# Half of the first layer of the last 1024 tokens as seven products in place of eight

## The chip, the cores and the metric

The kernel runs on one core of a Trainium2 chip. Its time is the device time of one execution in microseconds (us). The engines have short names: PE is TensorE (PEld its weight loads), DVE is VectorE, ACT is ScalarE, POOL is GpSimd, and SP is the engine that issues the DMAs.

## The reference

Attention with a sliding window of 32 tokens to either side, for 8 sequences of 576 tokens with 8 heads of 64, is followed by a feed-forward layer over all 4608 tokens:

```python
scores = scale * np.matmul(q, k.transpose(0, 1, 3, 2))
mask = np.abs(pos[:, None] - pos[None, :]) <= window
attn = softmax(np.where(mask, scores, -1e9))
x = np.matmul(attn, v)                  # -> (4608, 512)
h = x @ w_in                            # 512 -> 2048
r = np.maximum(h, 0.0)
out = (s * (r * r) + b) @ w_out         # 2048 -> 512
```

## The kernel before

**Tiles and stages.** The 4608 tokens are cut into 9 blocks of 512 (`NG`). The first three blocks are cut further (`SPLIT`), the last six are not. Attention goes by units of 128 keys (two tiles of 64); the last five sequences run as one long chain of units. A unit takes scores on PE (L828), an exponential on ACT (L856), a mask on DVE (L860), the products with v on PE (L886), and the normalization on DVE (L908 and L910). For the later units SP then transposes the normalized tile into `XT` by DMA (L934). `XT` holds the attention's result with the model's dimension on the partitions; it is a ring of 1536 tokens.

**First layer.** `s1(m, f0)` makes one f-tile (128 of the 2048 columns of w_in) of block `m`: four matmuls of 512 columns into one of the two banks `W` (L1149), a rectification by ACT from PSUM into `R1` (L1156), and, for each two f-tiles, a square by DVE into `GT` (L1162). There are two buffers `GT`, for blocks with even and odd numbers.

**Second layer.** `second(x)` already works by seven products in place of eight (the Strassen-Winograd scheme): the squares of a block and w_out are each taken as a 2 x 2 matrix, sums of the parts are made by DVE (L1198 for the squares, `weight_sums` once for w_out), and each product is two groups of eight matmuls of 256 columns (L1206) into the banks `O`. DVE adds each product, scaled by s, to the rows of the output (L1222), and SP stores them (L1231). The last block (`apart`) also uses the banks `SC`, which the attention no longer needs.

**The order of the work.** The kernel records each piece of work as a task with its engine, an estimated cost, what it reads and writes, and a due time `key`. A planner (`_Graph.plan`) then takes tasks one after the other, the earliest possible start first and the earlier key among equals, and so fixes one order for each engine, which the engine follows strictly. `_Graph.emit` adds the waits on semaphores. The keys come from a plan of stages: in stage x the first layer of block x (`P1`) alternates with the second layer of block x - 1 (`P2`); after the last stage comes the second layer of block 8. `due(c, u)` gives the key of an attention unit, some 14 us ahead of the block that needs it.

**Loads.** SP's queue holds the loads of q, k and v of the later sequences, the transposes of q and k (after POOL has cast them to bf16, L780, the transposes at L796), the transposes into `XT` (L934) and the stores (L1231), in the planner's order. v is cast to bf16 by ACT (L613) or DVE (L614) in turn. At the end `flag` tests that all row sums of the attention lie in a safe range, and only otherwise a slow general program runs.

The functions that the change touches, with the lines that the profile names:

Of the kernel before, what the change touches and what calls it, by code (L numbers as in the profile page):

```python
# [5 lines left out]
F32 = mybir.dt.float32  # L6
# [48 lines left out]
KEPT = 8  # L55
STIR = {("turn", 0, "q"): 7, ("scores", 0): 3, ("turn", 1, "q"): 2, ("turn", 1, "k"): 1, ("turn", 2, "q"): 1, ("turn", 2, "k"): 1,
# [267 lines left out]
def bass_sliding_window_symmetric__then__act_starrelu_kernel(  # L324
# [23 lines left out]
    with ExitStack() as es:  # L348
# [85 lines left out]
        for x in range(NG + 1):  # L434
            ms = BLOCKS[x] if x < NG else []
            n2 = 14 if x else 0
            work = sum(16 * c1(m) for m in ms)
            long, start = work + n2 * 0.874, at
            for m in ms:
                PH.append(at)  # L440
                share = long * 16 * c1(m) / work
                for ft in range(16):
                    P1[m, ft] = at + ft / 16.0 * share
                at += share
            for i in range(n2):
                P2[x - 1, i] = start + (i + 0.5) / n2 * long + (DELAY if x < NG else 0.0)
            at = start + long
# [23 lines left out]
        def due(c, u):  # L471
# [5 lines left out]
            before = PH[blk] - PH[blk - 1] if blk > 0 else 4.0  # L477
            return PH[blk] - 14.0 - (1.0 - f) * before
# [646 lines left out]
        def place(m):  # L1125

            return TBLK[m][0] // 512 % 2, TBLK[m][0] % 512

        def gt_res(gs, fc, c0, n):
            return [("GT", gs, fc, c) for c in range(c0 // 32, (c0 + n) // 32)]  # L1130
# [4 lines left out]
        def s1(m, f0):  # L1135
# [22 lines left out]
            if both and not half:  # L1158
# [3 lines left out]
            add("dve", lambda e: e.tensor_tensor(GT[gs][:, f1:f1 + nf, g0:g0 + nt], rr, rr, ALU.mult),  # L1162
                130 + 0.55 * nf * nt, reads=[("R1", rb, x) for x in range(2 if both else 1)],
                writes=[r for g in range(nf) for r in gt_res(gs, f1 + g, g0, nt)], key=key)

# [15 lines left out]
        def g_part(x, y, t):  # L1181
            return GT[x % 2].rearrange("p (g y) c -> p g y c", y=2)[:, :, y, HT * t:HT * t + HT]

        def g_res(x, y, t, halves=(0, 1)):
            return [r for h in halves for g in range(4 * h, 4 * h + 4) for r in gt_res(x % 2, 2 * g + y, HT * t, HT)]

        def second(x):
# [57 lines left out]
            for h in (0, 1):  # L1245
                k = P1[max(BLOCKS[x][-1], NE), 10] if h == 0 else key[0] - 1.0
# [57 lines left out]
        for x in range(1, NG):  # L1304
            for m in BLOCKS[x]:
                attend(m)
                for ft in range(0, 16, group(m)):
                    s1(m, ft)
            second(x - 1)
        second(NG - 1)  # L1310

        def flag():
# [3 lines left out]
            low, both = STG[0][:, 0:NU * H], STG[1][:, 0:NU * H]  # L1316
            low_res, both_res = stg_res(0, 2 * DM), stg_res(2 * DM, 2 * DM)
# [245 lines left out]
```

## Time and profile before

| | us |
|---|---|
| median of 3 runs | 307.87 |
| lowest, highest | 306.24, 308.62 |
| the profiled execution's own time | 309.07 |
| its span, from the first to the last instruction | 307.3 |

The profile shows one execution. Its page gives busy times by engine, a strip of 40 slices, the DMA queues, the chain of work that ended last, and the costliest groups of instructions. A row of a group gives the kernel's line, the engine, the operation, output and inputs, shapes and count, then busy time and the mean duration of one, then the idle time before them with what ended it. Matmuls overlap, so their single durations in a timeline are longer than what each adds; the chain of waits shows what a group adds.

### The profile page before, as it was taken

What the parts mean: (1) busy time and instruction counts of PE and PEld (TensorE: products, weight loads), DVE (VectorE), ACT (ScalarE), POOL (GpSimd) and SP (SyncE); (2) the same over time, 40 slices, a digit from 0 to 9 for tenths busy, and PEclk for the clock granted to TensorE, in tenths of its full rate; (3) what the DMA queues carried; (4) which work ended last, traced back from release to release, by engine and by line L of the source; (5) the groups of instructions that cost most, each with busy time, mean ns of one, the idle gap of its engine ahead of it and who ended that gap; (6) DMA issues with size and microseconds to landing.
All of it is one profiled execution on the core that took longest, in us unless ns stands there. A gap on an engine that the chain in (4) does not pass through costs nothing.

```text
span 307.3 us, 8802 instructions
## 1 busy us (share of the span) xinstructions
PE 292.1 (95%) x3822; PEld 211.1 (69%) x3849; DVE 230.2 (75%) x394; ACT 164.3 (53%) x261; POOL 63.3 (21%) x77
## 2 busy tenths in 40 slices
PE   8986899999999999999999999999899999999994
PEld 2455778798888887666766675666566666666784
DVE  4665798998769697977699897796876776566673
ACT  3754876695888564757465446543654433333300
POOL 5153568100000242037005400370000000000000
PEclk9999999999999999999999999999999999999999
DMA  6999999999793979999899879897803110200223
GB/s 182 316 265 319 310 288 359 285 246 229 172 194 94 246 136 163 251 236 210 158 286 200 158 178 258 191 184 141 237 17 87 53 47 22 83 30 6 69 70 107
DMA packets 118616, 54.43 MB, mean 177 GB/s; under 512 B 91232, under 2 KB 114400, under 8 KB 118576
## 3 DMA queue, kind: packets, MB, share of 16 engines
q1 hardware_dynamic: 118576, 53.85, 73.4%
q8 instruction: 31, 0.51, 0.7%
q14 instruction: 9, 0.07, 0.1%
HBM read 36.70 MB, written 9.44 MB: 150 GB/s over the span
## 4 chain that ended last, share of the span: by engine, by line
PE 78%; SPq 8%; DMA 5%; DVE 3%; issue 2%; POOL 2%; ACT 1%; POOLq 0%
PE w L1149 35%; PE o L1206 31%; DMA stg<-in_k_dram 4%; PE avn L886 4%; SPq L761 2%; PE sc L1206 2%; PE sc L828 2%; POOL nat L780 2%; SPq L796 1%; DMA vst<-in_v_dram 1%; SPq L650 1%; PE avn L917 1%; SPq L620 1%; SPq L577 1%; DVE kt L699 1%
## 5 line engine op out<-in xcount | busy, mean ns | idle before, releaser
L1149 PE MATMUL w<-xt,win 128*128 128x512 bf16 (+4 forms) x805 | 137.6, 312 | 3.8 <-issue 1.6
L1156 ACT ACTIVATE r<-w 128x512 bf16<-128x512 f32 (+2 forms) x148 | 86.2, 586 | 85.0 <-PE w L1149 82.5
L1149 PEld LDWEIGHTS w<-xt,win 128*128 128x128 bf16 x832 | 73.9, 98 | 34.9 <-ACT r L1156 1.3
L1162 DVE TENSOR_TENSOR gt<-r 128x1024 bf16<-128x1024 bf16 (+3 forms) x100 | 62.3, 629 | 31.4 <-ACT r L1156 30.9
L1206 PE MATMUL o<-wout,gt 128*128 128x256 bf16 x528 | 66.5, 273 | 0.0
L1206 PEld LDWEIGHTS o<-wout,gt 128*128 128x128 bf16 x528 | 50.9, 98 | 13.0
L780 POOL CAST nat<-stg 128x1024 bf16<-128x1024 f32 (+2 forms) x28 | 32.4, 1158 | 80.2 <-DMA stg<-in_q_dram 65.3
L856 ACT ACTIVATE ex<-sc 128x1024 bf16<-128x1024 f32 (+1 forms) x29 | 29.6, 1022 | 17.6 <-PE avn L886 16.3
L1206 PE MATMUL o<-tw,gt 128*128 128x256 bf16 x272 | 34.6, 273 | 0.0
L1222 DVE SCALAR_TENSOR_TENSOR outs<-o,sb,cvec 128x512 f32<-128x512 f32 (+1 forms) x36 | 25.7, 715 | 8.2 <-PE o L1206 7.9
L1206 PEld LDWEIGHTS o<-tw,gt 128*128 128x128 bf16 x272 | 26.3, 98 | 7.4
L1222 DVE SCALAR_TENSOR_TENSOR outs<-o,sb,outs 128x512 f32<-128x512 f32 (+1 forms) x27 | 19.3, 715 | 8.4 <-PE o L1206 8.3
L1198 DVE TENSOR_TENSOR gt<-gt 128x1024 bf16<-128x1024 bf16 (+1 forms) x26 | 23.7, 913 | 0.2
L860 DVE TENSOR_TENSOR ex<-ex,mask 128x1024 bf16<-128x1024 bf16 (+1 forms) x29 | 21.5, 740 | 1.4 <-ACT ex L856 0.9
L910 DVE TENSOR_TENSOR xn<-avn,rec 128x512 bf16<-128x512 f32 (+1 forms) x31 | 21.2, 685 | 0.5
L886 PE MATMUL avn<-vb,ex 64*64 64x65 bf16 x944 | 19.9, 197 | 0.3
L886 PEld LDWEIGHTS avn<-vb,ex 64*64 64x64 bf16 x944 | 12.9, 107 | 9.1 <-issue 4.7
L1206 PE MATMUL o<-tw,gsum 128*128 128x256 bf16 x136 | 17.6, 273 | 0.0
L1206 PEld LDWEIGHTS o<-tw,gsum 128*128 128x128 bf16 x136 | 13.1, 98 | 3.9
L1198 DVE TENSOR_TENSOR gsum<-gt 128x1024 bf16<-128x1024 bf16 x18 | 13.0, 721 | 0.4
L925 ACT COPY xt<-avn 128x512 bf16<-128x512 bf16 (+2 forms) x18 | 9.4, 531 | 4.9 <-PE avn L917 4.9
L828 PE MATMUL sc<-qt,kt 64*64 64x128 bf16 x440 | 11.7, 216 | 0.0
(132 smaller groups left out, 232.1 us busy)
## 6 DMA issues: line engine op xcount, KB each, us to landing
out_dram<-outs SPq DMA_DIRECT2D x32, 256.0 KB, 3.0
vst<-in_v_dram SPq DMA_DIRECT2D x28, 256.0 KB, 4.2
stg<-in_k_dram SPq DMA_DIRECT2D x24, 256.0 KB, 6.4
stg<-in_q_dram SPq DMA_DIRECT2D x5, 1024.0 KB, 6.5
stg<-in_moe_w_in_dram SPq DMA_DIRECT2D x8, 512.0 KB, 7.4
stg<-in_moe_w_out_dram SPq DMA_DIRECT2D x8, 512.0 KB, 7.3
stg<-in_q_dram SPq DMA_DIRECT2D x4, 512.0 KB, 8.9
stg<-in_k_dram SPq DMA_DIRECT2D x4, 512.0 KB, 8.9
```

The source lines that it names most:

```text
L780: (lambda e, dst=dst, src=src: e.tensor_copy(dst, src)),
L828: fns = [lambda e, pr=pr, x=x, b=b, j=j, hp=hp: e.matmul(SC[64 * x:64 * x + 64, hp, pr * 128:pr * 128 + 128], lhsT=k_tile(b, pr, j)[64 * h ...
L856: add("act", lambda e, dst=flat_dst, src=flat_src: e.activation(dst, src, AF.Exp, bias=0.0, scale=0.125), 190 + 0.833 * 512 * len(hs), rea ...
L860: add("dve", lambda e, flat=flat, mask=mask: e.tensor_tensor(flat, flat, mask, ALU.mult), 130 + 0.53 * 512 * len(hs), reads=[("E", ei, hp, ...
L886: return [lambda e: e.matmul(av[64 * x:64 * x + 64, h, 0:D + 1], lhsT=buf[64 * g:64 * g + 64, h % 2, h // 2, c:c + 64], rhs=VB[64 * g:64 * ...
L910: add("dve", lambda e: e.tensor_tensor(XN[xi][0:p1, :].rearrange("p (a c) -> p a c", a=H), av[0:p1, :, 0:D], REC[ri][0:p1, :].rearrange("p ...
L1149: add("pe", [lambda e, g=g, kc=kc: e.matmul(wt[:, g, :], lhsT=WIN_BF[:, kc, (f0 + g) * 128:(f0 + g + 1) * 128], rhs=XT[:, kc, t0 % XR:t0 % ...
L1156: add("act", lambda e: e.activation(rt, wt, AF.Relu, bias=0.0, scale=1.0), 190 + 0.833 * ng * nt, reads=[("W", wb)], writes=[("R1", rb, ha ...
L1162: add("dve", lambda e: e.tensor_tensor(GT[gs][:, f1:f1 + nf, g0:g0 + nt], rr, rr, ALU.mult), 130 + 0.55 * nf * nt, reads=[("R1", rb, x) fo ...
L1198: add("dve", lambda e: e.tensor_tensor(dst, x, y, op), 1240.0 if half is None else 690.0, reads=reads, writes=writes, key=k)
L1206: add("pe", [lambda e, g=g, j=j, dst=dst: e.matmul(dst, lhsT=lhs[:, g, 128 * j:128 * j + 128], rhs=rhs[:, g, :], start=first and g == 0 an ...
L1222: add("dve", lambda e, src=src, dst=dst, other=other: e.scalar_tensor_tensor(dst, src, SB128[:, 0:1], other, ALU.mult, ALU.add), 200 + 1.0 ...
```

## The change

For the f-tiles 8 to 15 of the last two blocks (7 and 8, 1024 tokens), the first layer is now made by `quad_group`, four times. A quad is two f-tiles by two blocks: the two halves of the model's dimension and two f-tiles of w_in make a 2 x 2 matrix, and the two halves and two blocks of `XT` make the other. Seven products of two matmuls each give the four results. Products 1, 6, 7 and 4 accumulate one on the other in one PSUM bank (`chain`), and after each of the first three ACT copies the partial sum to SBUF (`keep`). Products 2, 5 and 3 go to other banks (`other`, `side`); DVE adds a kept sum to them (`join`). ACT then rectifies, and DVE squares as before. `quad_sums` makes four sums of w_in (into `NAT`, keyed 8 us before the quads, and not before the attention product of the fifth unit from the end) and four of `XT` (into `VST`, when all attention is done), all by DVE.

The f-tiles 0 to 7 of both blocks stay with `s1`. All quads stand in stage 7, interleaved with the second layer of block 6, so stage 8 has only eight f-tiles left, and block 8 gets a third buffer of squares of its own, in the space of the staging buffers `STG`. The banks of the attention (`AVN`, `SC`) serve as chain and side banks, so the attention must be finished before; `due` gives the units of the last two blocks earlier keys. The sums of the last block's second layer and `flag` move to other buffers or keys.

The core of the diff:

```diff
@@ -53,6 +53,16 @@
 EV2 = ("act", "dve", "act", "dve", "act")
 
 KEPT = 8
+QUADS = 4
+FASTEST = 16 - 2 * QUADS
+TRAIL = 2.0
+FIN = 0.75
+LEAD = 7.0
+TURNS = ("dve", "dve") * QUADS
+HELD = 4
+AHEADS = 8.0
+AFTER = 5
+SUMS = ("dve", "dve")
 STIR = {("turn", 0, "q"): 7, ("scores", 0): 3, ("turn", 1, "q"): 2, ("turn", 1, "k"): 1, ("turn", 2, "q"): 1, ("turn", 2, "k"): 1,
         ("turn", 3, "q"): 1, ("turn", 3, "k"): 1, ("scores", 2): 1, ("scores", 3): 1, ("av", 0): 5, ("turn", "t"): 2}
 OUTSIDE = -1.0e38
@@ -434,16 +444,21 @@
         for x in range(NG + 1):
             ms = BLOCKS[x] if x < NG else []
             n2 = 14 if x else 0
-            work = sum(16 * c1(m) for m in ms)
+            fts = range(FASTEST) if x == NG - 1 else range(16)
+            quads = 28 * c1(NM - 1) / 4 * QUADS if x == NG - 2 else 0.0
+            work = sum((FASTEST if x >= NG - 2 else 16) * c1(m) for m in ms) + quads
             long, start = work + n2 * 0.874, at
             for m in ms:
                 PH.append(at)
-                share = long * 16 * c1(m) / work
-                for ft in range(16):
-                    P1[m, ft] = at + ft / 16.0 * share
+                share = long * ((FASTEST if x >= NG - 2 else 16) * c1(m) + quads) / work
+                for ft in fts:
+                    P1[m, ft] = at + ft / len(fts) * share * (FIN if x == NG - 1 else 1.0)
+                    if quads:
+                        P1[m, ft] = at + (ft * c1(m) if ft < FASTEST else FASTEST * c1(m) + (ft - FASTEST) / (16 - FASTEST) * quads) * long / work
+                        P1[m + 1, ft] = P1[m, ft] + 0.05
                 at += share
             for i in range(n2):
-                P2[x - 1, i] = start + (i + 0.5) / n2 * long + (DELAY if x < NG else 0.0)
+                P2[x - 1, i] = start + (i + 0.5) / n2 * long + (TRAIL if x == NG - 2 else DELAY if x < NG else 0.0)
             at = start + long
         PH.append(P2[NG - 1, 0] - 0.5 * n2 / 14 * 0.874)
         PH.append(at)
@@ -475,6 +490,8 @@
             blk = next(x for x in range(NM) if TBLK[x][0] + TBLK[x][1] > tok)
             f = (tok - TBLK[blk][0]) / TBLK[blk][1]
             before = PH[blk] - PH[blk - 1] if blk > 0 else 4.0
+            if blk >= NM - 2:
+                return PH[NM - 3] - LEAD + (tok - TBLK[NM - 2][0]) / 1024 * (P1[NM - 2, FASTEST] - PH[NM - 3])
             return PH[blk] - 14.0 - (1.0 - f) * before
 
 
@@ -1124,9 +1141,16 @@
 
         def place(m):
 
-            return TBLK[m][0] // 512 % 2, TBLK[m][0] % 512
+            return home(TBLK[m][0] // 512), TBLK[m][0] % 512
+
+        def home(x):
+            return 2 if x == NG - 1 else x % 2
+
+        GTS = GT + [STGS[:, 0:4096].bitcast(BF16).rearrange("p (f c) -> p f c", f=16)]
 
         def gt_res(gs, fc, c0, n):
+            if gs == 2:
+                return [("STG", 4 * fc + c) for c in range(c0 // 128, (c0 + n - 1) // 128 + 1)]
             return [("GT", gs, fc, c) for c in range(c0 // 32, (c0 + n) // 32)]
 
         def group(m):
@@ -1159,9 +1183,116 @@
                 return
             f1, nf = (f0 - 1, 2) if both else (f0, ng)
             rr = R1[rb][:, 0:nf * nt].rearrange("p (g c) -> p g c", g=nf)
-            add("dve", lambda e: e.tensor_tensor(GT[gs][:, f1:f1 + nf, g0:g0 + nt], rr, rr, ALU.mult),
+            add("dve", lambda e: e.tensor_tensor(GTS[gs][:, f1:f1 + nf, g0:g0 + nt], rr, rr, ALU.mult),
                 130 + 0.55 * nf * nt, reads=[("R1", rb, x) for x in range(2 if both else 1)],
                 writes=[r for g in range(nf) for r in gt_res(gs, f1 + g, g0, nt)], key=key)
+
+        quad, weight = {}, {}
+
+        def quad_sums():
+
+            x0, key = TBLK[NM - 2][0], P1[NM - 2, FASTEST]
+            c0 = x0 % XR
+            assert c0 + 1024 <= XR
+
...
+                for dst, a, b, op, reads, i in ((S1, a21, a22, ALU.add, [], 0), (S2, S1, a11, ALU.subtract, own[0], 1),
+                                                (S3, a11, a21, ALU.subtract, [], 2), (S4, a12, S2, ALU.subtract, own[1], 3)):
+                    eng = SUMS[part]
+                    add(eng, lambda e, dst=dst, a=a, b=b, op=op: e.tensor_tensor(dst, a, b, op),
+                        510.0 * n if eng == "pool" else 140.0 + 141.0 * n,
+                        reads=Win + reads, writes=own[i], key=P1[NM - 2, ft] - AHEADS + 0.1 * i,
+                        waits=[land["av", LONG, seq_units(LONG) - AFTER]])
+
...
+            B11, B12, B21, B22 = (XT[:, 2 * lower:2 * lower + 2, c0 + 512 * t:c0 + 512 * t + 512] for lower in (0, 1) for t in (0, 1))
+            T1, T2, T3, T4 = T
+            early, late_ = xt_res(x0, x0 + 512), xt_res(x0 + 512, x0 + 1024)
+            for dst, a, b, reads, i in ((T1, B12, B11, early + late_, 0), (T2, B22, T1, late_ + [("VST", 0)], 1),
+                                        (T3, B22, B12, late_, 2), (T4, B21, T2, early + [("VST", 1)], 3)):
+                add("dve", lambda e, dst=dst, a=a, b=b: e.tensor_tensor(dst, a, b, ALU.subtract), 700.0,
+                    reads=reads, writes=[("VST", i)], key=key - 2.0 + 0.1 * i)
+
...
+        def quad_group(i):
+
+            f0, z = FASTEST + 2 * i, i % 2
+            m = NM - 2
+            name, bank = (("AVN", AVN), ("SC", SC))[z]
+            wb = count["w"] % 2
+            count["w"] += 1
+            ra, rb = count["r"] % NR1, (count["r"] + 1) % NR1
+            count["r"] += 2
+            chain, side, other = ((name, 0), bank[:, 0, :]), ((name, 1), bank[:, 1, :]), (("W", wb), W[:, wb, :])
+            key = [P1[m, f0] + (P1[m, f0 + 1] - P1[m, f0]) * x / 3.5 for x in range(8)]
...
+            def product(n, dst, first, k):
+                (lhs, lres), (rhs, rres) = weight[i // HELD][n], quad[n]
+                add("pe", [lambda e, kk=kk: e.matmul(dst[1], lhsT=lhs(i % HELD, kk), rhs=rhs[:, kk, :], start=first and kk == 0, stop=(kk == 1),
+                                                     skip_group_check=True) for kk in (0, 1)],
+                    c1(m) * 500.0, reads=lres + rres, writes=[dst[0]], key=k, slack=XTS if n < 3 else 0.0)
+
+            def keep(dst, res, k):
+                add("act", lambda e: e.copy(dst, chain[1]), 617.0, reads=[chain[0]], writes=res, key=k)
+
+            def join(src, mine, res, r, half, k):
+                add("dve", lambda e: e.tensor_tensor(R1[r][:, 512 * half:512 * half + 512], src[1], mine, ALU.add), 660.0,
+                    reads=[src[0]] + res, writes=[("R1", r, half)], key=k)
+
+            def rectify(dst, src, reads, r, halves, k):
+                add("act", lambda e: e.activation(dst, src, AF.Relu, bias=0.0, scale=1.0), 190 + 0.833 * 512 * len(halves),
+                    reads=reads, writes=[("R1", r, x) for x in halves], key=k)
+
+            def square(r, t, eng, k):
+                gs = home(NG - 2 + t)
+                rr = R1[r][:, :].rearrange("p (g c) -> p g c", g=2)
+                add(eng, (lambda e: e.activation(GTS[gs][:, f0:f0 + 2, :], rr, AF.Square, bias=0.0, scale=1.0)) if eng == "act" else
+                    (lambda e: e.tensor_tensor(GTS[gs][:, f0:f0 + 2, :], rr, rr, ALU.mult)), 700.0 if eng == "dve" else 1040.0,
+                    reads=[("R1", r, x) for x in (0, 1)], writes=[x for g in (0, 1) for x in gt_res(gs, f0 + g, 0, 512)], key=k)
+
+            A, C = R1[ra], R1[rb]
+            product(1, chain, True, key[0])
+            keep(p1, p1r, key[0])
+            product(2, other, True, key[1])
+            product(6, chain, False, key[2])
+            keep(u2, u2r, key[2])
+            join(other, p1, p1r, ra, 0, key[1])
+            product(5, side, True, key[3])
+            product(7, chain, False, key[4])
+            keep(u3, u3r, key[4])
+            join(side, u3, u3r, rb, 1, key[4])
+            product(3, side, False, key[5])
+            join(side, u2, u2r, rb, 0, key[5])
+            product(4, chain, False, key[6])
+            rectify(A[:, 0:512], A[:, 0:512], [("R1", ra, 0)], ra, (0,), key[3])
+            rectify(C[:, :], C[:, :], [("R1", rb, x) for x in (0, 1)], rb, (0, 1), key[6])
+            rectify(A[:, 512:1024], chain[1], [chain[0]], ra, (1,), key[6])
+            square(rb, 1, TURNS[2 * i], key[7])
+            square(ra, 0, TURNS[2 * i + 1], key[7])
 
         def weights_part(y, c0):
             return WOUT_BF.rearrange("p (g y) c -> p g y c", y=2)[:, :, y, c0:c0 + HN]
@@ -1179,10 +1310,10 @@
                     reads=reads, writes=writes, key=key)
 
         def g_part(x, y, t):
-            return GT[x % 2].rearrange("p (g y) c -> p g y c", y=2)[:, :, y, HT * t:HT * t + HT]
+            return GTS[home(x)].rearrange("p (g y) c -> p g y c", y=2)[:, :, y, HT * t:HT * t + HT]
 
         def g_res(x, y, t, halves=(0, 1)):
-            return [r for h in halves for g in range(4 * h, 4 * h + 4) for r in gt_res(x % 2, 2 * g + y, HT * t, HT)]
+            return [r for h in halves for g in range(4 * h, 4 * h + 4) for r in gt_res(home(x), 2 * g + y, HT * t, HT)]
 
         def second(x):
 
@@ -1243,7 +1374,7 @@
                 s2, s4 = (STG[i].bitcast(BF16).rearrange("p (g c) -> p g c", g=8) for i in (4, 5))
                 rs2, rs4 = (stg_res(2 * DM * i, 2 * DM) for i in (4, 5))
             for h in (0, 1):
-                k = P1[max(BLOCKS[x][-1], NE), 10] if h == 0 else key[0] - 1.0
+                k = P1[max(BLOCKS[x][-1], NE), 10 if x < NG - 1 else FASTEST - 1] if h == 0 else key[0] - 1.0
                 h11, h12, h21, h22 = (g_res(x, y, t, (h,)) for t in (0, 1) for y in (0, 1))
                 total(s1, a21, a22, ALU.add, h21 + h22, [("GSUM", h)], k, h)
                 if apart:
@@ -1304,8 +1435,13 @@
         for x in range(1, NG):
             for m in BLOCKS[x]:
                 attend(m)
-                for ft in range(0, 16, group(m)):
+                for ft in range(0, 16 if x < NG - 2 else FASTEST, group(m)):
                     s1(m, ft)
+            if x == NG - 2:
+                attend(NM - 1)
+                quad_sums()
+                for i in range(QUADS):
+                    quad_group(i)
             second(x - 1)
         second(NG - 1)
 
@@ -1313,8 +1449,8 @@
 
             key = PH[-2] - 24.0
             seen = RECS.rearrange("p u h -> p (u h)")
-            low, both = STG[0][:, 0:NU * H], STG[1][:, 0:NU * H]
-            low_res, both_res = stg_res(0, 2 * DM), stg_res(2 * DM, 2 * DM)
+            low = both = VST[:, 4, :, :].rearrange("p h d -> p (h d)")[:, 0:NU * H]
+            low_res = both_res = [("VST", 4)]
             add("dve", lambda e: e.tensor_scalar(low, seen, LEAST, None, ALU.is_ge), 450,
                 reads=[("REC", i) for i in range(NU)], writes=low_res, key=key)
             add("dve", lambda e: e.scalar_tensor_tensor(both, seen, 1.0 / LEAST, low, ALU.is_le, ALU.mult), 450,
```

23 lines of the change are left out of this document (added).

## The prediction, made before the result was known

> **What bounds the kernel now.** I read the page first, then the windows of the last 100 us, the chain of waits, and the timelines of the engines.
>
> ```profile
> span 307.3 us, 8802 instructions
> ```
>
> ```profile
> core 0: us, PE busy (x) PEld busy (x) DVE busy (x) ACT busy (x) POOL busy (x), PEclk, DMA share, GB/s
> ...
> 210.00:220.00 10.00, 8.68 (x147) 5.80 (x147) 6.92 (x12) 4.96 (x8) 0.00 (x0) 1.00 0.79 190
> 220.00:230.00 10.00, 9.95 (x111) 6.49 (x110) 7.41 (x13) 4.80 (x9) 0.00 (x0) 1.00 0.24 59
> 230.00:240.00 10.00, 9.79 (x147) 6.73 (x147) 7.37 (x13) 4.90 (x7) 0.00 (x0) 1.00 0.26 67
> 240.00:250.00 10.00, 9.77 (x87) 6.43 (x87) 7.39 (x13) 3.58 (x6) 0.00 (x0) 1.00 0.21 55
> 250.00:260.00 10.00, 9.95 (x68) 6.56 (x68) 6.36 (x11) 3.61 (x7) 0.00 (x0) 1.00 0.07 24
> ```
>
> From 216 us on TensorE is the bound: 98 to 99% busy at a granted clock of 1.00, with VectorE at 64 to 74%, ScalarE at 36 to 49%, GpSimd idle and DMA at 0.07 to 0.26. So a matmul taken away there is time saved, as long as VectorE and ScalarE can carry what replaces it. The one hole near the change lies in 210 to 220. The chain names it:
>
> ```profile
> 211.05 3.83 DMA vst<-in_v_dram
> 214.91 0.62 ACT vb L613
> 215.52 0.51 ACT r L1156
> ...
> 217.99 0.25 PE avn L886 x16
> ...
> 218.79 0.81 PE w L1149 x3
> ...
> 228.18 1.73 PE w L1149 x8
> 229.91 0.87 PE o L1206 x8
> ```
>
> ```profile
> 216.07 1.04 PE L1149 MATMUL w<-xt,win 128*128 128x512 bf16 x4 [1.05 <-ACT r L1156]
> ```
>
> A load of v is issued after the last transposes of k, ScalarE's cast stands waiting for it, the rectifications queue behind the cast, and TensorE finds both W banks full: 1.05 us lost. The later rows give the unit prices: an attention unit takes TensorE from 217.99 to 218.79, 0.8; a first-layer matmul of 512 columns takes 1.73/8 = 0.216 us of TensorE, a first-layer group of four 0.87, a second-layer group of eight 0.87.
>
> **The products.** For f-tiles 8 to 15 of blocks 7 and 8 the change removes 2 x 8 x 4 = 64 such matmuls and adds 4 quads x 7 products x 2 = 56 of the same shape (0.43 us a product). That is 8 x 0.216 = 1.73 us less of TensorE. Weight loads fall by the same eight and are hidden anyway (64 to 67% busy above, while TensorE computes). This is the whole direct gain.
>
> **What ScalarE gets.** It loses 16 rectifications and gets, per quad, three copies of a partial sum out of PSUM (512, to f32), two rectifications of 512 and one of 1024.
>
> ```profile
> L1156 ACT ACTIVATE r<-w 128x512 bf16<-128x512 f32 x45 | 26.7, 597 | 41.5 <-PE w L1149 40.3 <-PE avn L1324 1.1
> L856 ACT ACTIVATE ex<-sc 128x1024 bf16<-128x1024 f32 x3 | 3.1, 1023 | 2.0 <-PE avn L886 1.9
> ```
>
> An f32 copy isn't in the trace: at least 0.60 (same size, bf16 out), at most 1.02 (twice the elements); I take 0.60, since only the output type differs. Four quads: 12 x 0.60 + 8 x 0.60 + 4 x 1.02 = 16.1 us, 6.5 more than the 16 x 0.60 it replaces; at 1.02 a copy, 21.1. ScalarE has half its time free. What matters is the order inside a quad: products 1, 6, 7, 4 accumulate in one bank, and the next may write only when the copy of the last is made. In the built order at least a second-layer group and one product stand between two of these, 0.87 + 0.43 = 1.30 us, against a copy of 0.60 (margin about 0.65) or 1.02 (0.25). So I cost the copies at nothing; the second-layer groups hide them. Without that cover each would cost up to 0.60, twelve of them 7 us.
>
> **What VectorE gets.** It keeps as many squares and gets 12 joins (PSUM plus f32), 4 sums of w_in and 4 of the attention's result, each of 1024 in bf16.
>
> ```profile
> L1162 DVE TENSOR_TENSOR gt<-r 128x1024 bf16<-128x1024 bf16 x23 | 15.9, 691 | 16.1 <-ACT r L1156 15.9
> L1222 DVE SCALAR_TENSOR_TENSOR outs<-o,sb,cvec 128x512 f32<-128x512 f32 x11 | 8.2, 745 | 3.5 <-PE o L1206 3.5
> L1198 DVE TENSOR_TENSOR gsum<-gt 128x1024 bf16<-128x1024 bf16 x6 | 4.1, 686 | 0.1
> L910 DVE TENSOR_TENSOR xn<-avn,rec 128x512 bf16<-128x512 f32 x4 | 2.8, 689 | 0.1
> L1198 DVE TENSOR_TENSOR gt<-gsum,gt 128x2048 bf16<-128x2048 bf16 x2 | 2.4, 1216 | 0.0
> ```
>
> A join lies between L910 (0.69: PSUM and f32 in, bf16 out) and L1222 (0.745: f32 out); I take 0.69, its nearest form. The sums are L1198's form, 0.69. So 20 x 0.69 = 13.8 us more for VectorE. The full durations overlap when the queue is full:
>
> ```profile
> 217.78 0.69 DVE L1162 TENSOR_TENSOR gt<-r 128x1024 bf16<-128x1024 bf16 x1
> 218.39 0.74 DVE L1222 SCALAR_TENSOR_TENSOR outs<-o,sb,outs 128x512 f32<-128x512 f32 x1
> 219.05 0.20 DVE L908 RECIPROCAL rec<-avn 128x8 f32<-128x8 f32 x1
> ```
>
> A square of 0.69 is followed after 0.61, an eviction of 0.74 after 0.66: 0.08 less each. (The Trainium skill, "VectorE: DVE Perf Modes", Terms, says that the pipe is flushed after every VectorE operation and the next can't issue before it is empty. Read as charging whole durations, that is against this change; the starts in these rows lie closer together than the durations, so the measurement decides.)
>
> **The critical hand-over.** All attention of the last two blocks must now be finished before the quads. In the built order the last attention product follows the first unit of the last sequence by 23 groups and 5 units, 23 x 0.87 + 5 x 0.8 = 24 us; now it is 34.5 later (first row below to the second). After the last attention product come 24 groups and 28 products, 24 x 0.87 + 28 x 0.43 = 33.0 us to the end of the last quad; 11.3 of these stand before product 6, the first that needs a sum of the attention's result. VectorE has to normalize, SP to transpose, and VectorE to make the sums, and these stand in its queue ahead of squares and evictions. Today's last unit shows the steps:
>
> ```profile
> 210.73 0.32 PE L886 MATMUL avn<-vb,ex 64*64 64x65 bf16 x16
> ...
> 245.24 0.70 PE L886 MATMUL avn<-vb,ex 64*64 64x65 bf16 x24
> ```
>
> ```profile
> 246.02 0.20 DVE L908 RECIPROCAL rec<-avn 96x8 f32<-96x8 f32 x1
> 246.26 0.69 DVE L910 TENSOR_TENSOR xn<-avn,rec 96x512 bf16<-96x512 f32 x1
> ```
>
> ```profile
> 246.97 1.18 SPq L934 DMA_TRANSPOSE xt<-xn  x1
> ...
> DMA to landing us min/median/max: 2.3/3.0/5.6
> ```
>
> From the product's end (245.94) to the normalized tile 1.0, and 0.7 for a sum that now stands between; landing 3.0 after the issue's start or (if counted from its end) 4.2: the sums start 4.7 to 5.9 us after the last product. Three of them take 3 x 0.61 + 0.08 = 1.9, so product 6 has them at 6.6 to 7.8, and it is due at 11.3. From its first sum to its last join VectorE has 27 operations of 0.69, 7 evictions of 0.745, two double sums of 1.2 and 0.6 of the flag's, 26.9 us in whole durations, 38 x 0.08 = 3.0 less back to back, so 23.9; there are 33.0 less 4.7 to 5.9 for it, 27.1 to 28.3. The margin is 3.2 to 4.4, or 0.2 to 1.4 in whole durations. I take 1 us, near the lower, since VectorE also has to await each product inside a quad. So the normal landing costs nothing. The w_in sums (2.8 us) lie in the 24 us before: 5 units of 1.6, 6 squares, 6 evictions, sums of 4.0 and these make 23.7 in whole durations, 20.9 back to back; tight, and hidden by what TensorE has there.
>
> **SP and the hole at 215.** No DMA is added. SP's order changes: now one more load of v (the third of the last sequence's five) is issued ahead of that sequence's transposes, and two stand behind them, one for a cast by VectorE. ScalarE's cast that waited until 214.88 finds its data. At best the 1.05 goes; at worst VectorE, or the cast of the fifth, waits as long in its place and nothing is won. I take half, 0.5.
>
> **The sum.** Profiled execution 309.07 us (span 307.3, 1.77 around it): 309.07 - 1.73 - 0.5 = 306.84. The median of the three runs, 307.87, is 1.20 lower, so 307.87 - 2.23 = **305.6 us**.
>
> **Rivals.**
> - *No gain.* The last transposes land as late as the slowest in the rows, 5.6 instead of 3.0. VectorE waits 2.6 longer at the head of its queue, 1 is covered, 1.6 goes to TensorE and eats the 1.73: 307.87 - 1.73 + 1.6 = 307.7. For it: VectorE has 23.9 us of work for 27 there. Against: little else moves by DMA then (0.07 to 0.26 above).
> - *Slower.* The last transposes stand in SP's queue behind stores, which wait for VectorE's evictions, and VectorE waits for the transposes. A transpose behind such a store waited up to 4.0 us:
>
> ```profile
> SPq L934 <- DVE outs L1222: 6.8, 3, 4.0
> ```
>
> 4.0 less 1 is 3.0 for TensorE: 309.1; with a landing of 5.6 too, 5.6 for TensorE: 311.7. It decides from 2.7 us of lateness (1 + 1.73). Against it: in the built order the store ahead of the last transpose belongs to an eviction that VectorE makes before it normalizes.
> - *More.* The hole goes whole, 307.87 - 2.78 = 305.1, and the execution falls low in the scatter of the runs (306.24 to 308.62, so 0.8 either way): 304.3 to 304.8.
> - *The products don't shorten the stage*, because ScalarE becomes its bound: with copies at 1.02 its 21.1 us and five rectifications of the blocks between (3.0) are 24.1, against 26 products and 12 groups of TensorE from product 2 of the first quad to the last, 11.3 + 10.4 = 21.7. That costs 2.4: 305.6 + 2.4 = 308.0. For it: nobody has timed the copy. Against: its nearest row is 0.60. I count it with "no gain".
>
> **How the numbers follow.** Forecast (305.1 to 306.4) 0.50; more 0.20; no gain 0.14; slower 0.16. A change of 1% (3.1 us) is about what a measurement of this kernel can tell from none. Faster by over 1% is below 304.8: the rival "more" and a tenth of the forecast, 0.25. Slower by over 1% is above 310.9: about three quarters of "slower", its long landings and some scatter, 0.12. The rest is 0.63. The range reaches from 304.3 (hole gone, 0.8 of scatter) to 309.1 (the middle of "slower"); the forecast's own with scatter is 304.3 to 307.2.
>
> **What would show it.** Right: 56 matmuls of the new line, 8 fewer in all; TensorE still 98% busy in the windows from 216 to the end; the hole before 216 smaller; the copies followed by the next product of their bank without a wait on ScalarE; the tail after the last product as now. Wrong: TensorE idle inside the quads with VectorE's joins or ScalarE's copies as releaser, VectorE idle over 3 us at the first sum of the attention's result, or a new wait for a v cast before 220.

## The result, and the profile after

The changed kernel took 304.69 us (median), the kernel before beside it 307.59; the ratio is 0.9928, 95% interval 0.9903 to 0.9952. On the 307.87 of the prediction that is 2.2 us less, with an interval of 1.5 to 3.0; the prediction said 2.23 less (305.6 us). The ratio counts fast executions alone and so is nearer to 1 than the ratio of the two medians, 0.9906 (2.9 us).

The windows of the profiled execution, from the same places as before (columns: PE, PEld, DVE, ACT, POOL busy, the granted clock, the DMA share, GB/s):

```profile
span 304.7 us, 8843 instructions
```

```profile
core 0: us, PE busy (x) PEld busy (x) DVE busy (x) ACT busy (x) POOL busy (x), PEclk, DMA share, GB/s
210.00:220.00 10.00, 9.67 (x154) 6.61 (x153) 7.59 (x13) 5.35 (x8) 0.00 (x0) 1.00 0.89 178
220.00:230.00 10.00, 10.00 (x154) 6.52 (x153) 9.23 (x18) 5.06 (x8) 0.00 (x0) 1.00 0.32 79
230.00:240.00 10.00, 9.93 (x125) 6.56 (x123) 8.24 (x16) 3.90 (x6) 0.00 (x0) 1.00 0.30 79
240.00:250.00 10.00, 10.00 (x64) 6.08 (x63) 8.44 (x15) 5.41 (x10) 0.00 (x0) 1.00 0.14 38
250.00:260.00 10.00, 10.00 (x68) 6.48 (x67) 8.33 (x13) 5.49 (x10) 0.00 (x0) 1.00 0.08 26
```

TensorE stays full, and VectorE, 64 to 74% busy before, has 82 to 92% from 220 us on. TensorE's waits from 172 us to the end:

```profile
PE w L1173 <- ACT r L1180: 0.6, 1, 0.6
PE avn L903 <- DMA kt<-nat: 0.5, 1, 0.5
PE avn L903 <- issue: 0.3, 1, 0.3
```

All three lie before the quads (at 176.7, 190.1 and 213.0). Inside the quads, and from there to the end, the profile lists no wait of TensorE. The groups of the new work:

```profile
L1260 ACT COPY stg<-avn 128x512 f32<-128x512 f32 x6 | 3.5, 585 | 1.9 <-PE avn L1255 1.9
L1267 ACT ACTIVATE r<-r 128x1024 bf16<-128x1024 bf16 x4 | 4.2, 1059 | 0.6 <-DVE r L1263 0.6
L1263 DVE TENSOR_TENSOR r<-w,stg 128x512 bf16<-128x512 f32 x4 | 2.7, 687 | 0.9 <-PE w L1255 0.9
L1217 DVE TENSOR_TENSOR nat<-win 128x1024 bf16<-128x1024 bf16 x2 | 1.4, 688 | 0.0
L1232 DVE TENSOR_TENSOR vst<-xt 128x1024 bf16<-128x1024 bf16 x2 | 1.3, 688 | 0.8 <-DMA xt<-xn 0.8
```

The estimates stand: 0.585 for a copy (0.60), 0.687 for a join (0.69), 0.688 for a sum (0.69). The hand-over, from the timelines of PE and DVE:

```profile
236.70 0.71 PE L903 MATMUL avn<-vb,ex 64*64 64x65 bf16 x24
...
248.61 0.59 PE L1255 MATMUL avn<-vst,nat 128*128 128x512 bf16 x2
```

```profile
242.66 1.29 DVE L1232 TENSOR_TENSOR vst<-xt 128x1024 bf16<-128x1024 bf16 x2 [0.80 <-DMA xt<-xn]
243.87 0.68 DVE L1232 TENSOR_TENSOR vst<-xt,vst 128x1024 bf16<-128x1024 bf16 x1
```

The last attention product ends at 237.41. The first sum starts 5.25 us later (4.7 to 5.9 was forecast), after VectorE has idled 0.80. Product 6 (at 248.61) comes 11.2 us after that end (11.3), and its sum is ready at 244.55, 4.06 us before it.

For a comparison without the scatter of the early, DMA-bound part, I measure from a place that both kernels pass (the first attention product of the unit at 174 to 180 us) to the start of the last group of the second layer. Times in us from the PE timelines:

| execution | first product of the unit | last attention product | last group | stretch |
|---|---|---|---|---|
| before | 177.32 | 245.24 | 302.41 | 125.09 |
| before, second profile | 174.40 | 242.82 | 299.99 | 125.59 |
| after | 176.69 | 236.70 | 299.95 | 123.26 |
| after, second profile | 175.55 | 234.51 | 297.76 | 122.21 |
| before, with after's early attention alone | 174.38 | 233.35 | 298.33 | 123.95 |

In the last stage, from the last attention product to the last group, both profiles of after take the same 63.25 us; they differ only ahead of it.

### The profile page after: what moved, and what is told of

Its sections match the earlier page's. It is cut to its first block, busy times and chain, and to the rows that moved or that the text cites. A ratio compares the mean times of both kernels' runs of the same rounds, so it can differ in the third digit from the quotient of the medians.

```text
span 304.7 us, 8843 instructions
## 1 busy us (share of the span) xinstructions
PE 292.9 (96%) x3841; PEld 210.1 (69%) x3841; DVE 238.4 (78%) x414; ACT 169.6 (56%) x269; POOL 63.9 (21%) x77
## 4 chain that ended last, share of the span: by engine, by line
PE 61%; DMA 23%; SPq 6%; POOL 4%; DVE 2%; issue 1%; ACT 1%; POOLq 0%
PE o L1337 27%; PE w L1173 21%; DMA stg<-in_moe_w_out_dram 6%; DMA vst<-in_v_dram 5%; DMA stg<-in_q_dram 5%; DMA stg<-in_k_dram 4%; SPq L778 4%; POOL nat L797 3%; DMA stg<-in_moe_w_in_dram 3%; PE avn L903 2%; PE sc L1337 2%; DMA kt<-nat 2%; PE sc L1255 2%; PE avn L1255 2%; SPq L813 2%; PE sc L845 1%
## 5 line engine op out<-in xcount | busy, mean ns | idle before, releaser
L1173 PE MATMUL w<-xt,win 128*128 128x512 bf16 (+4 forms) x768 | 127.8, 308 | 0.8 <-ACT r L1180 0.6
L1180 ACT ACTIVATE r<-w 128x512 bf16<-128x512 f32 (+2 forms) x132 | 76.6, 585 | 69.6 <-PE w L1173 69.1
L1173 PEld LDWEIGHTS w<-xt,win 128*128 128x128 bf16 x768 | 67.8, 98 | 30.3 <-issue 1.2
L1186 DVE TENSOR_TENSOR gt<-r 128x512 bf16<-128x512 bf16 (+3 forms) x88 | 52.5, 604 | 17.4 <-ACT r L1180 17.2
L1337 PE MATMUL o<-wout,gt 128*128 128x256 bf16 x512 | 64.5, 273 | 0.0
L1337 PEld LDWEIGHTS o<-wout,gt 128*128 128x128 bf16 x512 | 49.3, 98 | 12.8 <-DVE outs L1353 0.4
L1337 PE MATMUL o<-tw,gt 128*128 128x256 bf16 x256 | 32.6, 273 | 0.0
L1337 PEld LDWEIGHTS o<-tw,gt 128*128 128x128 bf16 x256 | 24.7, 98 | 6.6
L630 ACT CAST vb<-vst 128x512 bf16<-128x512 f32 (+1 forms) x16 | 9.9, 617 | 5.8 <-DMA vst<-in_v_dram 5.8
L1329 DVE TENSOR_TENSOR gsum<-gt 128x1024 bf16<-128x1024 bf16 x16 | 12.0, 750 | 0.6 <-PE o L1337 0.3
```

The costliest lines, as they stand in the source:

```text
L1173: add("pe", [lambda e, g=g, kc=kc: e.matmul(wt[:, g, :], lhsT=WIN_BF[:, kc, (f0 + g) * 128:(f0 + g + 1) * 128], rhs=XT[:, kc, t0 % XR:t0 % ...
L1180: add("act", lambda e: e.activation(rt, wt, AF.Relu, bias=0.0, scale=1.0), 190 + 0.833 * ng * nt, reads=[("W", wb)], writes=[("R1", rb, ha ...
L1186: add("dve", lambda e: e.tensor_tensor(GTS[gs][:, f1:f1 + nf, g0:g0 + nt], rr, rr, ALU.mult), 130 + 0.55 * nf * nt, reads=[("R1", rb, x) f ...
L1329: add("dve", lambda e: e.tensor_tensor(dst, x, y, op), 1240.0 if half is None else 690.0, reads=reads, writes=writes, key=k)
L1337: add("pe", [lambda e, g=g, j=j, dst=dst: e.matmul(dst, lhsT=lhs[:, g, 128 * j:128 * j + 128], rhs=rhs[:, g, :], start=first and g == 0 an ...
```

## The experiments

Line numbers shift by a few where an edit adds lines: products of the quads are L1255 in after, L1258 in the late sums, L1257 in the copies.

**The eighth product put back.** In `quad_group`:

```diff
             product(5, side, True, key[3])
+            product(5, side, True, key[3])
```

Product 5 is computed twice, in vain; order and all else stay.

> The changed kernel with product 5 of each quad made twice (same result, 4 x 2 = 8 matmuls of 512 columns more), so the first layer has as many matmuls as before, while the moved attention, the copies, joins and sums all stay. Theory (the saving is the eight matmuls of 0.216 us, TensorE being the bound there): 1.7 us above the changed kernel, some 0.5 us below the kernel before, and from the first quad on TensorE stays over 98% busy. Rival (the gain comes from the moved attention and loads, TensorE has room in the quads): within 0.5 us of the changed kernel, with idle time of TensorE in the quads filled.

Measured: 306.63 us, ratio 0.996 (0.9919 to 1.0002). That is 1.0 us above after by the ratios, but the two intervals overlap, so the times alone don't decide. The profiled execution (310.87 us) is the longest of its kernel, so I read only its last stage, which has a granted clock of 1.00 and no waits (first two lines; the third line is the last group of after):

```profile
239.41 0.70 PE L903 MATMUL avn<-vb,ex 64*64 64x65 bf16 x24
...
304.39 1.04 PE L1338 MATMUL o<-tw,stg 128*128 128x256 bf16 x8
```

```profile
299.95 1.04 PE L1337 MATMUL o<-tw,stg 128*128 128x256 bf16 x8
```

That is 64.98 us from the last attention product to the last group, against 299.95 - 236.70 = 63.25 in after: eight matmuls are worth 1.73 us there, the forecast's number. The rival falls with it: TensorE had no idle time in the quads to fill.

**The early attention alone.** The kernel before, with the due times that after's rule gives, and no quads:

```diff
+            if blk >= NM - 2:
+                return PH[NM - 3] - 7.0 + (tok - TBLK[NM - 2][0]) / 1024 * (P1[NM - 2, 6] - PH[NM - 3])
             return PH[blk] - 14.0 - (1.0 - f) * before
```

> The kernel before with only the due times of the last 1024 tokens' attention moved as in the change; no quads, no extra sums. Its orders of SP and of the three compute engines equal the changed kernel's up to the last attention product. Theory: only the hole of 1.05 us before 216 us moves, so between 0 and 1 us below the kernel before (0.5 expected). Rival (the moved attention is the gain): 2 us below it, like the whole change.

Measured: 307.61 us, ratio 0.9978 (0.9943 to 1.0014); no gain that the times can tell (0.7 us, between a loss of 0.4 and a gain of 1.8). The rival of 2 us lies outside that. Its profiled execution has no wait of TensorE over 0.2 us in the stretch, 123.95 us. Against it the two profiles of before lose 1.14 and 1.64. After's second profile, also without such a wait, has 122.21, 1.74 less: the products again. Its last stage is 64.98 us, as long as the one with the eighth product put back:

```profile
233.35 0.70 PE L888 MATMUL avn<-vb,ex 64*64 64x65 bf16 x24
...
298.33 1.04 PE L1208 MATMUL sc<-tw,gt 128*128 128x256 bf16 x8
```

**The sums of w_in on GpSimd.**

```diff
-SUMS = ("dve", "dve")
+SUMS = ("pool", "pool")
```

> The changed kernel with the four sums of w_in made by GpSimd, which is idle then, in place of VectorE. Theory (VectorE carries these 2.8 us beside TensorE at no cost): no change, within 0.4 us, VectorE 2.8 us less busy in 215 to 235. Rival (VectorE is too full late in the attention): 0.5 to 1.5 us faster. Second rival (GpSimd's sums slow VectorE's operations beside them, as when it casts: the sum at 206.5 us took 1.40 in place of 0.69): VectorE's operations in that stretch over 0.8 us each, and up to 1 us slower.

Measured: 306.62 us, ratio 0.9958 (0.9921 to 0.9996), where after has 0.9928. The timelines of POOL, then of DVE beside it:

```profile
216.08 4.73 POOL L1217 TENSOR_TENSOR nat<-win 128x1024 bf16<-128x1024 bf16 x2 [9.42 <-PE avn L903]
220.89 2.98 POOL L1217 TENSOR_TENSOR nat<-nat,win 128x1024 bf16<-128x1024 bf16 x1
223.95 2.45 POOL L1217 TENSOR_TENSOR nat<-win,nat 128x1024 bf16<-128x1024 bf16 x1
```

```profile
218.75 0.74 DVE L1353 SCALAR_TENSOR_TENSOR outs<-o,sb,outs 128x512 f32<-128x512 f32 x1
...
221.82 0.68 DVE L927 TENSOR_TENSOR xn<-avn,rec 128x512 bf16<-128x512 f32 x1
222.42 2.00 DVE L877 TENSOR_TENSOR ex<-ex,mask 128x1024 bf16<-128x1024 bf16 x1
224.34 2.60 DVE L1186 TENSOR_TENSOR gt<-r 128x1024 bf16<-128x1024 bf16 x1
226.87 0.74 DVE L1353 SCALAR_TENSOR_TENSOR outs<-o,sb,cvec 128x512 f32<-128x512 f32 x1
```

A sum that VectorE makes in 0.69 takes GpSimd 2.4 to 3.0, and meanwhile VectorE's squares and masks take 2.0 to 2.6 in place of 0.69. VectorE's queue came late by several of these, and the mask at 222.42, the last of them, made TensorE wait (4.06 us, in an execution some 5 us above its kernel's median, so the kind is shown and not the usual size). VectorE's evictions (0.74) and normalizations (0.68), which have one input in PSUM, stay as they are. The first profile of after has the same in a smaller measure beside GpSimd's casts: a sum of 1.40 in place of 0.69 (POOL, then DVE), and the normalization after it as ever:

```profile
202.44 5.96 POOL L797 CAST nat<-stg 128x1024 bf16<-128x1024 f32 x5 [2.12 <-DMA stg<-in_k_dram]
```

```profile
206.53 1.40 DVE L1329 TENSOR_TENSOR gsum<-gt 128x1024 bf16<-128x1024 bf16 x1
207.85 0.68 DVE L927 TENSOR_TENSOR xn<-avn,rec 128x512 bf16<-128x512 f32 x1
```

The Trainium skill, "SBUF — State Buffer", Who interferes with whom, has this rule: a VectorE instruction with two inputs from SBUF contends with a GpSimd instruction that reads SBUF, one with at most one such input, outside the 2-port modes, doesn't. The rows agree. So the second rival's mechanism is there, and nothing speaks for the first (faster by 0.5 to 1.5 us). Whether the time changes stays open: that GpSimd costs time against after is likely, but the two intervals overlap.

**Six quads.**

```diff
-QUADS = 4
+QUADS = 6
```

> The changed kernel with six quads in place of four (f-tiles 4 to 15 by seven products). Theory (each quad saves two matmuls as long as VectorE and ScalarE keep up): 4 x 0.216 = 0.87 us faster than the changed kernel. Rival (VectorE, with 6 more joins and 4 more sums of w_in, 10 x 0.61 us back to back, becomes the bound of the quads): 0 to 3 us slower than it, with TensorE waiting for joins.

Measured: 305.39 us, ratio 0.9925 (0.9891 to 0.996): no gain against four quads that the times can tell, though the interval is too wide to exclude the 0.87. Its waits of TensorE from 170 us on, in the PE timeline (gaps of 0.16, which the waitless profiles have too, left out):

```profile
192.81 1.90 PE L1173 MATMUL w<-xt,win 128*128 128x512 bf16 x8 [0.18 <-ACT r L1180]
...
206.27 1.89 PE L1173 MATMUL w<-xt,win 128*128 128x512 bf16 x8 [0.49 <-issue]
...
211.55 0.32 PE L903 MATMUL avn<-vb,ex 64*64 64x65 bf16 x16 [0.78 <-DMA kt<-nat]
...
287.91 1.92 PE L1337 MATMUL o<-tw,gt 128*128 128x256 bf16 x16 [0.42 <-DVE outs L1353]
```

Its stretch is 299.27 - 175.31 = 123.96 us; without waits it would be 122.21 - 0.87 = 121.34. The rows name 1.87 of the 2.6 lost. The attention, due earlier still, waits for transposes of k; and at 287.91 an eviction came late because VectorE made the last block's sums ahead of it. The rest fits what the next two pairs show: a wait costs more than the gap that the profile gives it. This is one profile, and the waits ahead of the quads also differ between the two profiles of four quads; only the wait at 287.91 has no like in any profile of four or five. No wait is for a join, so the rival as it was put isn't what happened.

**The margin of VectorE.** Four and eight more sums of the attention's result, into unused space, ahead of the first:

```diff
-                add("dve", lambda e, dst=dst, a=a, b=b: e.tensor_tensor(dst, a, b, ALU.subtract), 700.0,
-                    reads=reads, writes=[("VST", i)], key=key - 2.0 + 0.1 * i)
+                more = [lambda e, a=a, b=b, j=j: e.tensor_tensor(MORE[j].rearrange("p (k c) -> p k c", k=2), a, b, ALU.subtract) for j in range(4)] if i == 0 else []
+                add("dve", more + [lambda e, dst=dst, a=a, b=b: e.tensor_tensor(dst, a, b, ALU.subtract)], 700.0,
+                    reads=reads, writes=[("VST", i)] + spare, key=key - 2.0 + 0.1 * i)
```

> VectorE makes four more sums of the attention's result, into space that nothing reads, right ahead of the first one; the order of every engine is otherwise that of after. In the trace of after, sums start 0.605 us apart, so the rest of VectorE's queue comes 4 x 0.605 = 2.4 us later. Theory A (the prediction's margin of 1 us): the narrow place isn't the sums' own reader but the second join of the first quad, which frees the side bank: in after it ends at 252.60 and product 3 writes the bank at 253.39, 0.79 later, and VectorE idles 0.28 in between, 1.07 in all; TensorE waits 1.3 to 1.4 us for DVE r at L1263 or thereabouts and the kernel is that much longer. Theory B (the backlog margin of 3.2 to 4.4 us, or the 4.1 us that the trace of after shows between the second sum's end at 244.55 and product 6 at 248.61): no wait of TensorE, no time.

> Eight more sums ahead of the first one, 4.8 us. Theory A (1.07 us of margin at the side bank): TensorE waits 3.8 us in all, part of it at product 6 (0.8, the direct slack of 4.1 being used up), the rest at product 3 of the first quad. Theory B (3.2 to 4.4 of margin): 0.4 to 1.6 us. Theory C (every later join has its own slack and the queue catches up in VectorE's idle gaps): 0.8, at product 6 alone.

These two kernels and the next two ran once each (306.01 and 307.16 us, then 303.96 and 310.76; before beside them 306.92), which is too few for the times to tell anything; I compare the last stage in the traces. The PE timelines, every wait from the last attention product to the end, of four more and then of eight more:

```profile
250.93 0.60 PE L1258 MATMUL avn<-vst,win 128*128 128x512 bf16 x2 [0.18 <-ACT stg L1263]
...
252.79 0.60 PE L1258 MATMUL avn<-xt,nat 128*128 128x512 bf16 x2 [0.38 <-DVE r L1266]
```

```profile
246.39 0.61 PE L1258 MATMUL avn<-vst,nat 128*128 128x512 bf16 x2 [0.43 <-DVE vst L1235]
...
252.10 0.60 PE L1258 MATMUL avn<-vst,win 128*128 128x512 bf16 x2 [1.84 <-ACT stg L1263]
...
253.96 0.61 PE L1258 MATMUL avn<-xt,nat 128*128 128x512 bf16 x2 [0.38 <-DVE r L1266]
```

The stage from the last attention product to the last group is 64.17 us (235.20 to 299.37) and 66.65 (233.88 to 300.53), against 63.25: 0.92 and 3.40 us lost. From four to eight the loss grows by 2.48, as much as the lateness (2.42), so the margin is 2.42 - 0.92 = 1.5 or 4.84 - 3.40 = 1.4. Theory A has the size nearly (1.07 of margin, losses of 1.35 and 3.8), and theories B and C are out. The place is only half right. The side bank's join at L1266 is there (0.38), but more is lost one step earlier, by way of ScalarE. Its timeline with four more sums:

```profile
249.77 0.63 ACT L1270 ACTIVATE r<-r 128x512 bf16<-128x512 bf16 x1 [1.44 <-DVE r L1266]
250.31 0.56 ACT L1263 COPY stg<-avn 128x512 f32<-128x512 f32 x1
```

A rectification stands in ScalarE's queue waiting for VectorE's first join, and the third copy, for which product 4 waits, stands behind it.

**The margin of ScalarE.** One and two more copies (to bf16) into unused space ahead of each of the twelve:

```diff
-                add("act", lambda e: e.copy(dst, chain[1]), 617.0, reads=[chain[0]], writes=res, key=k)
+                more, spare = [], []
+                for _ in range(1):
+                    j = uses["more"] % len(MORE)
...
+                    more.append(lambda e, j=j: e.copy(MORE[j], chain[1]))
...
+                add("act", more + [lambda e: e.copy(dst, chain[1])], 617.0, reads=[chain[0]], writes=res + spare, key=k)
```

> Each of ScalarE's twelve copies is preceded by one more copy of the same bank into space that nothing reads; the order is that of after. A copy took 0.585 and the next instruction of ScalarE started 0.49 after its start, so the hand-over to the next product comes 0.49 later. Theory A (the prediction: a margin of 0.65 between the copy and the next product of its bank; in the trace of after 0.52 to 0.55 at six of the twelve, 0.95 to 1.6 at the others): covered, 0 to 0.1 us at each of the six, 0 to 0.5 us in all. Rival (the copies are already on the path, covered only by what the trace can't show): 12 x 0.49 = 5.9 us.

> Two more copies ahead of each, 0.98 us. Theory A: the six narrow places (0.52 to 0.55) each lose 0.43 to 0.5, so TensorE waits 2.6 to 3.0 us for ACT at L1260, and the gain of the seven products is gone. Rival (ScalarE has as much again to spare, since a stall at one copy makes the next one earlier): about half of it, 1.3 to 1.5 us.

With one more, TensorE shows no wait in the quads and the stage is 63.62 us (233.63 to 297.25), 0.37 more than 63.25. With two more it is 67.91 (236.57 to 304.48), 4.66 more. Its PE timeline has these waits:

```profile
250.73 0.60 PE L1257 MATMUL avn<-vst,nat 128*128 128x512 bf16 x2 [0.35 <-ACT stg L1268]
...
252.99 0.60 PE L1257 MATMUL avn<-vst,win 128*128 128x512 bf16 x2 [0.35 <-ACT stg L1268]
...
257.42 0.60 PE L1257 MATMUL sc<-vst,nat 128*128 128x512 bf16 x2 [0.35 <-ACT nat L1268]
...
264.06 0.60 PE L1257 MATMUL avn<-vst,nat 128*128 128x512 bf16 x2 [0.35 <-ACT stg L1268]
...
266.47 0.60 PE L1257 MATMUL avn<-vst,win 128*128 128x512 bf16 x2 [0.50 <-ACT stg L1268]
...
271.29 0.60 PE L1257 MATMUL sc<-vst,nat 128*128 128x512 bf16 x2 [0.71 <-ACT nat L1268]
```

Its ACT timeline at the first of these places:

```profile
249.11 1.07 ACT L1266 CAST stg<-avn 128x512 bf16<-128x512 f32 x2 [0.27 <-PE avn L1257]
250.07 0.60 ACT L1268 COPY stg<-avn 128x512 f32<-128x512 f32 x1
```

Two more copies take 0.96 us (249.11 to 250.07). The product after them starts with a gap of 0.35, and all that follows comes 0.51 later than in after, counted from the last attention product: the overlap of 0.16 between one matmul and the next is lost too. So the margin at the narrow places is 0.96 - 0.51 = 0.45, and it fits the other run, where one more copy (0.48) costs 0.03 to 0.04 at four of the narrow places and 0.17 at a fifth. The prediction had 0.65. Theory A has the six places, which lose 3.6 us together; its sum of 2.6 to 3.0 was too low by this overlap and because the later copies also queue behind ScalarE's rectifications (0.50 and 0.71 at the end). The other 1.0 of the 4.66 comes at four starts for which the profile lists no gap. Two of them follow a copy (261.80 and 273.69). The other two, at 261.06 and 274.42, are product 3 behind a join of VectorE that itself waited for a copy, a path that theory A didn't have:

```profile
260.32 0.69 DVE L1271 TENSOR_TENSOR r<-sc,nat 128x512 bf16<-128x512 f32 x1 [0.67 <-ACT nat L1268]
```

The rivals (5.9 with one more, 1.3 to 1.5 with two) are out.

**Five quads**, `QUADS = 5`, and both kernels profiled once more:

> Five quads in place of four: f-tiles 6 to 15. Two matmuls fewer than after, 0.43 us. VectorE gets three joins and four narrow sums of w_in (256 columns) more, some 3.2 us; the attention of the last two blocks is due earlier. Theory A (the cost of six quads was that earlier attention waits for transposes of k and that the last block's sums come ahead of evictions, both growing with the number of quads): half of six quads' loss, so no better than after, within 0.4 us. Theory B (six quads ran over an edge that five don't reach): 0.43 us faster than after, a ratio to before of 0.9914.

> The kernel before, profiled once more, to see whether its hole of 1.05 us at 216 comes in every execution. Theory A (the order of SP's queue makes it: the load of v stands behind the transposes): a wait for ACT r of 0.9 to 1.2 us near 216 again. Theory B (it scatters with what the DMA does in that execution): between 0 and 0.5, or elsewhere.

> The changed kernel, profiled once more. Theory A: the waits of 0.64 at 190 and 0.33 at 213 come again, and none after 213. Theory B (scatter): between 177 and 213 the waits of TensorE sum to another value, 0 to 1.1 us; none after the last attention product in either theory, so that from its start to the last product's end there are 64.3 us.

Five quads: 303.71 us beside 307.23, ratio 0.9896 (0.9862 to 0.9931). Of the three numbers of quads it has the lowest ratio, 3.2 us below before, and its interval leaves out 1; but it overlaps that of four (0.9903 to 0.9952), so the times don't show that five are better than four. Its one trace speaks for theory B. From 172 us on it names only `issue` and `ACT r` gaps of at most 0.2, and its stretch is 295.25 - 173.68 = 121.57 us, 0.64 less than after's second profile, of which two matmuls are 0.43. VectorE is at 80 to 92% from 210 us to the end of the first layer, for instance:

```profile
250.00:260.00 10.00, 9.95 (x67) 6.48 (x67) 9.21 (x17) 6.36 (x12) 0.00 (x0) 1.00 0.01 2
260.00:270.00 10.00, 9.95 (x60) 5.72 (x60) 8.05 (x13) 7.43 (x12) 0.00 (x0) 1.00 0.23 79
```

Before's second profile has the hole again, longer, by the same chain (the cast waits for the load, the rectifications stand behind it); its ACT and PE timelines:

```profile
212.49 0.62 ACT L613 CAST vb<-vst 128x512 bf16<-128x512 f32 x1 [2.62 <-DMA vst<-in_v_dram]
```

```profile
213.66 1.04 PE L1149 MATMUL w<-xt,win 128*128 128x512 bf16 x4 [1.29 <-ACT r L1156]
```

After's second profile has neither the wait at 190 nor that at 213, and its last stage is as long as in the first (63.25). So theory A holds for before as to the cause (the wait of 1.29 is a little over the 0.9 to 1.2 expected), and theory B for after.

## Why the prediction was right

The forecast was 2.23 us less and the ratio gives 2.2. That they agree to 0.03 is luck, since the interval reaches from 1.5 to 3.0; what the runs bear out is the larger term and the mechanism.

- *The products, 1.73.* Measured 1.73 (eighth product put back) and 1.74 (early attention alone against after's second profile, neither with waits over 0.2).
- *The hole, "I take half, 0.5".* The reason was right: a load of v too late for ScalarE's cast, and a new order of SP that moves it. Before lost 1.14 and 1.64 us of its stretch to waits, after 1.05 and 0.0 (123.26 and 122.21 against 122.21). The gain of one execution against another lies between 0.1 and 1.6, so no single profile could show it: in the two first profiles it is only 0.1, and most of the rest of their difference beyond the products lies ahead of 177 us. The kernels with more sums and copies have after's order up to the last attention product, so their traces widen the sample. From the first product of the unit to the last attention product they take 59.92, 58.74, 59.25 and 59.87, after itself 60.01 and 58.96. Against the shortest, after's order lost 0.7 in the mean; before's two, measured by the same yardstick (123.95 less 0.23), lost 1.37 and 1.87. That makes a gain of 0.9 in the mean, from two executions against six; the times of the early attention alone say 0.7, between a loss of 0.4 and a gain of 1.8. So half a hole was a guess on the low side that the scatter covers. The wait that took its place came earlier (190), not at 215; VectorE's cast there did wait, 1.56 us, and cost nothing:

```profile
217.26 0.43 DVE L631 CAST vb<-vst 128x512 bf16<-128x512 f32 x1 [1.56 <-DMA vst<-in_v_dram]
```

- *ScalarE's copies, nothing; margin 0.65.* They cost nothing, but the margin measured 0.45: the subtraction 1.30 - 0.60 left out that the matmuls overlap by 0.16 and that a copy starts only at the last matmul's end. One more copy of 0.48 cost 0.37 in the stage, where a margin of 0.65 would have hidden it. The rival with copies of 1.02 is out (0.585). A rectification from SBUF takes 1.059 for 1024 columns, not 1.02, with no effect.
- *VectorE's margin, "I take 1 us, near the lower".* Measured 1.4 to 1.5. The reason for the low choice (VectorE must await each product inside a quad) was right, and the backlog margin of 3.2 to 4.4 is not what TensorE has. The path by ScalarE's rectification wasn't seen, so the size of the margin is nearly right and the place only in part.
- *Sums of w_in, nothing.* TensorE shows no wait after 213; VectorE was 92% busy in 220 to 230 and carried them. (The terms of the 23.7 us that the prediction gives for the stretch add up to 23.4, which changes nothing.)
- *Back-to-back VectorE, 0.08 less each.* Two sums took 1.29 and the third started 1.21 after the first: 0.605 apart at 0.685 each. The same measurement decides against the rule of the Trainium skill ("VectorE: DVE Perf Modes", Terms) as the prediction read it.
- *The rivals.* "No gain" needed a landing of 5.6 that comes at the end; the sums started 5.25 after the last product, within the normal case. "Slower" would have decided from 2.7 us of lateness; by the runs it is 1.45 + 1.73 = 3.2, and with eight more sums (4.84 us of lateness) the last stage is 66.65, 1.67 longer than the 64.98 with eight products. "More" (304.3 to 304.8) isn't what the ratio gives, 305.65 on the prediction's 307.87 (304.9 to 306.4), though it is close: by the two medians it would be 305.0. The plain median of 304.69 falls into its range only because before was lower beside it too.

## What to carry to other kernels

When one engine is full and the others are not, price what is taken off it by its own rows, and put the care into the hand-overs: for each, find the narrowest place in the order (here 0.45 us behind a copy, 1.4 to 1.5 behind a join). A subtraction of durations gave 0.65 for the one, and the sum of free time 3.2 to 4.4 for the other. Such a margin can be measured by making the producer do its work once more into unused space, with the order kept. And take several profiles before giving a single hole a price: its length, and the waits that took its place, differed between executions of the same kernel. More of a good thing isn't always more: six quads showed no gain over four, and brought a late eviction that no profile of four or five has.

## What the runs showed of the hardware that I had not expected

- A wait of TensorE in the quads cost more than the gap that the profile shows: in the kernel with two more copies, gaps of 0.35 delayed all that followed by 0.51 to 0.53 each, and with four more sums 0.18 and 0.38 made 0.92 together. The durations of matmuls overlap their successors' by 0.16 (0.59 for a product that adds 0.433), and at a wait this overlap is lost too. The four gaps of six quads, 1.87 and 4 x 0.16 more, make 2.51 of the 2.6 lost.
- A sum that VectorE makes in 0.69 us took GpSimd 2.4 to 3.0 beside a busy VectorE (none ran alone here), and slowed VectorE's own operations of two SBUF inputs to as much as 2.60 in place of 0.69.
- ScalarE copies 512 columns from PSUM in 0.585 to f32, no slower than a rectification to bf16 (0.597), and starts the next copy 0.46 to 0.49 after the last.
